# A gated update x + LN(x) y, written as one product (x - mean)(1 + rs y) with the row means put back later

## Chip, core and metric

The kernel runs on one core of a Trainium2 chip. The metric is the device time of one execution in microseconds (us), lower is better. Engines: PE (TensorE), DVE (VectorE), ACT (ScalarE), POOL (GpSimd), and SP, which only issues transfers.

## The reference, cut to what matters

Four residual layers alternate, A, B, A, B, on x of 2048 rows and 512 channels:

```python
x = A_q
x = x + _A_ref(_layernorm(x), A_k, A_v, A_shift_k, A_ssm_k, A_ssm_D)   # q * y
x = x + _B_ref(_layernorm(x), B_log_A_real, ...)                        # long convolution
x = x + _A_ref(_layernorm(x), A_k, A_v, A_shift_k, A_ssm_k, A_ssm_D)
x = x + _B_ref(_layernorm(x), B_log_A_real, ...)
```

`_layernorm` subtracts the row's mean and divides by the root of its variance plus 1e-5. `_A_ref(q, ...)` is `q * y`, where y depends on k, v and the filters and not on x, so it is the same in both A layers. `_B_ref(u, ...)` convolves u along the 2048 rows, channel by channel, with taps made from the B parameters, and adds `u * D_skip`.

So layer A is, for each row, x + (x - m) rs y with the row's mean m and rs = 1/sqrt(var + eps): a *gated update*.

## The kernel before

x lies in the on-chip memory as 16 tiles of 128 rows by 512 channels, `x[:, t, :]`. The text calls a tile a row `t`. The phases in order of time:

1. *Constants, A's y, and B's taps.* Two streams of work are interleaved. One (`diagonal`) computes A's y by long convolutions and writes it to memory (`ya_d`). The other (`taps`, `spectrum_quarter`) makes B's taps: for 64 steps an angle product on PE (L478, L483), an absolute value, a sine and a cosine on ACT (L491, L492, L493, written to tiles `tt`), products on DVE (L505, L506) and POOL (L504, L508), and a contraction on PE (L519, `pk`). Every fourth step writes taps out (L528, L529, L531, `kdram`). They are read back (L226), get D_skip added (L236), and are transformed (L171, L191, L196) into spectra `spec`, which go out from tiles `pc` (L244, L245).
2. *First gated update* (`gated_update(..., 0, True)`), which overlaps the last taps. It loads x (L701) and y (L703, tiles `yaq`, four rows each, three buffers for four loads, so the fourth load waits until the first buffer has been read).
3. *First B convolution* (`conv_b(0)`): normalised rows `u` (L770 on DVE or POOL, L773 on ACT) for one quarter of the channels at a time, forward transform on PE (L171), transposes on DVE (L189, L191), the second transform step on PE (L196, banks `pu`), whose result ACT reads out (L276, L277, tiles `sw`), products with the spectrum on DVE and POOL (L278, L280, L281), the inverse on PE (L290, L311), and the addition to x (L811, L813).
4. *Second gated update* (`gated_update(..., 1)`), which stands alone: the statistics of x end just ahead of it, and the normalisation for the next convolution follows it.
5. *Second B convolution* (`conv_b(1)`), which writes the output.

In the gated update before, each row takes a first step (x - m) y in one of three ways, chosen by a letter in WAYS1 or WAYS2: "c" is one DVE instruction (L714); "b" subtracts the mean on ACT (L717) and "d" on POOL (L719), and both then multiply by y on POOL (L720). L721 on DVE then forms ut rs + x and sums the row in the same instruction. L723 on ACT squares (sum - 512 x) and sums that, which gives the variance without another pass on DVE. `normalizer` turns the sums into nm (minus the mean), rs and nb (minus mean times rs): L208 and L209 on DVE, the root L210 on ACT, L211 to L216 on DVE. It is called once for rows 0 to 7 and once for rows 8 to 15. From row 8 on in the second update, a matmul without use (L727) keeps PE running.

The normalisation u = rs x + nb follows on three engines by letter tables (NORM1, NORM2 for the first quarter of channels, NORMQ for the second, ACT for the rest). The rows of the first three quarters are normalised before ACT reads out the first `pu`.

The order of each engine's instructions is not that of the source: a scheduler puts them in order by a simulated timeline, and each engine then works through its own list in that order. On ACT, roots, exponentials and sines need different tables; a change of kind is an ACT_TABLE_LOAD.

## Time and profile before

| | us |
|---|---|
| median of 3 runs (range) | 800.36 (798.78 to 801.9) |
| the profiled execution | 805.59 |
| its span, first to last instruction | 803.8 |
| busy in the span: PE, DVE, POOL, ACT | 635.2, 621.3, 533.7, 477.7 |
| first gated update, L717's first instruction to the last rows' normalisation | 466.1 to 523.6 |
| second gated update, first `nm` to the second `nb` | 662.3 to 693.0 |
| first read-out of `pu` (L276) behind it | 703.2 |

In the profile's rows, `out<-in` names tiles, `x8` counts instructions that were merged, and times are from the start of the span.

### The profile page before, as it was taken

The page shows a single profiled execution, that of the slowest core. Times are in us where ns is not written, and L with a number is a line of the kernel's source. Part 1 is how long each engine was busy: PE and PEld are TensorE (multiplying, and loading weights), DVE is VectorE, ACT ScalarE, POOL GpSimd, SP SyncE. Part 2 cuts the span into 40 slices and gives each one's busy share as a digit, 9 for nine tenths or more (in the row PEclk, how much of TensorE's full clock was granted, in tenths as well). Part 3 has the DMA queues.
Part 4 walks back from the last instruction along what each step waited for, and adds up shares of the span by engine and source line. Part 5 has one row for each costly group of instructions (what it writes and reads, how often), then busy time and mean ns, then how long its engine had stood idle before and what let it go on. Part 6 is the DMA issues. An engine that isn't in the chain of part 4 may idle for free. (4 is left out here: it accounts for less than half of the span.)

```text
span 803.8 us, 14448 instructions
## 1 busy us (share of the span) xinstructions
PE 635.2 (79%) x5064; PEld 447.3 (56%) x5064; DVE 621.3 (77%) x939; ACT 477.7 (59%) x879; POOL 533.7 (66%) x496
## 2 busy tenths in 40 slices
PE   3378696688799989999889863599789750998996
PEld 2255565356567747767556442386657620476673
DVE  7757979998967967647759499845668889878776
ACT  4035355345378875776785765649746525878573
POOL 4965778776778965838956277316665836288783
PEclk9676599868999999999899665789989995899999
DMA  9577177367477463664441593147987642068792
GB/s 326 188 247 270 40 241 254 108 200 254 146 215 203 127 182 110 182 171 123 115 131 34 174 341 105 46 129 199 233 200 183 159 103 54 1 164 223 201 252 105
DMA packets 89612, 135.47 MB, mean 169 GB/s; under 512 B 8508, under 2 KB 37700, under 8 KB 89028
## 3 DMA queue, kind: packets, MB, share of 16 engines
q1 hardware_dynamic: 88644, 132.13, 56.5%
q0 software_dynamic: 896, 2.43, 1.1%
q8 instruction: 40, 0.66, 0.4%
q14 instruction: 32, 0.26, 0.1%
HBM read 98.87 MB, written 35.65 MB: 167 GB/s over the span
## 5 line engine op out<-in xcount | busy, mean ns | idle before, releaser
L280 POOL TENSOR_TENSOR sw<-sw,kab 128x512 f32<-128x512 f32 x96 | 124.4, 1302 | 67.6 <-ACT sw L277 59.6
L196 PEld LDWEIGHTS pu<-zu,w 128*128 128x128 f32 x768 | 95.7, 193 | 52.9 <-DVE vv L278 18.6
L196 PE MATMUL pu<-zu,w 128*128 128x128 f32 x768 | 109.5, 285 | 15.1 <-DVE vv L278 12.8
L504 POOL TENSOR_TENSOR xy<-tt,m 128x512 f32<-128x512 f32 x64 | 84.9, 1327 | 53.5 <-ACT tt L493 23.8
L171 PE MATMUL pf<-kk,wz 128*128 128x256 f32 x256 | 86.3, 481 | 41.8 <-POOL kk L236 25.3
L278 DVE TENSOR_TENSOR vv<-pu,kab 128x512 f32<-128x512 f32 x96 | 64.9, 679 | 63.9 <-ACT sw L277 27.0
L290 PE MATMUL pi<-vv,mm 128*128 128x128 f32 x768 | 107.3, 285 | 3.5 <-DVE vv L278 2.6
L281 POOL TENSOR_TENSOR vv<-vv,sw 128x512 f32<-128x512 f32 x76 | 98.8, 1303 | 13.6 <-DVE vv L278 10.3
L290 PEld LDWEIGHTS pi<-vv,mm 128*128 128x128 f32 x768 | 96.5, 197 | 15.0 <-issue 9.1
L276 ACT ACTIVATE sw<-pu 64x512 f32<-64x512 f32 x96 | 57.0, 594 | 63.3 <-PE pu L196 60.8
L171 PEld LDWEIGHTS pf<-kk,wz 128*128 128x128 f32 x256 | 56.7, 237 | 62.3 <-POOL kk L236 33.3
L491 ACT ACTIVATE tt<-pa 128x512 f32<-128x512 f32 x64 | 38.3, 599 | 82.1 <-PE pa L483 72.3
L196 PE MATMUL pu<-zk,w 128*128 128x128 f32 x512 | 78.3, 307 | 6.4 <-DVE zk L191 4.2
L196 PEld LDWEIGHTS pu<-zk,w 128*128 128x128 f32 x512 | 72.7, 217 | 15.6 <-DVE zk L191 6.3
L505 DVE TENSOR_TENSOR tt<-tt,m 128x512 f32<-128x512 f32 x64 | 79.9, 1248 | 0.9 <-ACT tt L493 0.4
L244 ACT COPY pc<-pu 128x512 f32<-128x512 f32 x64 | 37.4, 591 | 57.3 <-PE pu L196 35.3
L506 DVE SCALAR_TENSOR_TENSOR xy<-tt,m 128x256 f32<-128x256 f32 x64 | 51.5, 805 | 25.7 <-ACT tt L492 15.3
L468 ACT ACTIVATE m<-pm 128x512 f32<-128x512 f32 x96 | 53.8, 604 | 22.6 <-PE pm L466 21.6
L483 PE MATMUL pa<-y,minus 128*128 128x512 f32 x64 | 37.1, 588 | 32.0 <-DVE y L482 30.5
L311 PE MATMUL po<-w,w 128*64 128x512 f32 x192 | 55.4, 655 | 7.3 <-DVE w L305 7.0
L519 PE MATMUL pk<-xy,tt 128*32 128x64 f32 x2048 | 50.5, 242 | 13.3 <-DVE ks L529 9.0
L519 PEld LDWEIGHTS pk<-xy,tt 128*32 128x32 f32 x2048 | 37.7, 122 | 39.1 <-issue 28.9
(139 smaller groups left out, 1295.4 us busy)
## 6 DMA issues: line engine op xcount, KB each, us to landing
kab<-spec SPq DMA_DIRECT2D x188, 256.0 KB, 4.0
spec<-pc SPq DMA_DIRECT2D x64, 256.0 KB, 2.7
kvt<-kv_in SPq DMA_DIRECT2D x16, 624.0 KB
yaq<-ya_d SPq DMA_DIRECT2D x8, 1024.0 KB, 10.6
kk<-ssmk_in SPq DMA_DIRECT2D x16, 256.0 KB, 2.9
kv_d<-u SPq DMA_DIRECT2D x16, 256.0 KB, 7.5
kdram<-ks SPq DMA_DIRECT2D x64, 64.0 KB, 1.8
kk<-kdram SPq DMA_DIRECT2D x16, 256.0 KB, 2.7
```

The lines of the kernel that those rows point to most:

```text
L171: yield T.matmul(o, w, rhs, start=True, stop=True)
L196: ins = T.matmul(pu[:, i, :], w2[:, c * CK + i, :], z[:, :, c * CK + i, :], start=True, stop=True)
L276: S.mul(sw[0:64], pu[64:128], -1.0)
L278: V.tensor_mul(vv, pu, kabs[s][:, 0])
L280: (V if last else G).tensor_mul(sw, sw, kabs[s][:, 1])
L281: (V if last or s % add_dve == add_dve - 1 else G).tensor_add(vv, vv, sw)
L290: i1s[t] = T.matmul(pi[:, i, :], mm[:, c * CK + i, :], vvs[t][:, i, :], start=True, stop=True)
L311: ins = T.matmul(po[64 * a:64 * a + 64], w4, ws[g][:, :, 16 * a:16 * a + 16, :].rearrange("p x t r -> p t x r"), start=True, stop=True, ti ...
L468: i = S.activation(m, pm, AF.Exp)
L504: G.tensor_mul(xy[:, :, :, 32:64], tt[:, :, :, 1:33], m1[:, :, 32:64][:, None].to_broadcast([128, 2, 8, 32]))
L505: (G if (4 * gi + k) % E2P == E2P - 1 else V).tensor_mul(e2, e2, m2[:, None].to_broadcast([128, 2, 8, 32]))
L519: T.matmul(pk[32 * i4:32 * i4 + 32, 2 * k + i, :], e2[:, r, 4 * i + i4, :], xy[:, r, 4 * i + i4, :], start=r == 0, stop=r == 1, tile_posit ...
```

## The change

The update is rewritten. (x - m)(1 + rs y) equals x - m + (x - m) rs y, that is, the wanted row less its mean. So per row ACT makes a factor 1 + rs y (one instruction, L718 of the changed file), and DVE makes one product (x + nm) times the factor and sums the row in the same instruction (L729). A normalisation does not see a constant added to a row, so the missing mean matters only where x itself is added to: it is collected in `off` (the sum of both updates' means) and put back once, on ACT, in the second convolution, when the third quarter's rows are due (L787, whole rows, 128x512). The third and fourth quarters are then normalised from the restored row, with a shifted nb (`nb2`, two POOL instructions).

The statistics: in the first update all 16 rows keep the square on ACT (L735). In the second, rows 0 to 7 do, and rows 8 to 15 use DVE's statistics instruction instead (L737, `BN = (16,8)`). Three factors are made ahead (`GA = 3`). The letter tables WAYS1 and WAYS2 are gone, and with them L714, L717, L719 and L720.

```diff
-    WAYS1 = "cbcdcbcdcbcdcbcd"
-    WAYS2 = "bcdbcbcbbcbbcbcb"
+    GA = 3
+    BN = (16,8)
...
+    off = cpool.tile([128, 16], F32, name="off")
...
+        groups = lambda a: a.rearrange("p (g c) -> p g c", c=32)
+        uts = {}
+        def factor(t):
+            pool, tag, bufs = spare[t % len(spare)]
+            uts[t] = pool.tile([128, 512], F32, name="ut", tag=tag, bufs=bufs)
+            S.activation(groups(uts[t]), yas[t // 4][:, :, t % 4, :], AF.Identity, scale=rs[:, t:t + 1], bias=1.0)
+
+        if rnd == 0:
+            G.tensor_scalar(off, nm, -1.0, None, op0=ALU.mult)
+        else:
+            for t0 in range(0, 16, HN):
+                G.tensor_sub(off[:, t0:t0 + HN], off[:, t0:t0 + HN], nm[:, t0:t0 + HN])
+        for t in range(GA):
+            factor(t)
         for t in range(16):
-            pool, tag, bufs = spare[t % len(spare)]
-            ut = pool.tile([128, 512], F32, name="ut", tag=tag, bufs=bufs)
-
-            groups = lambda a: a.rearrange("p (g c) -> p g c", c=32)
-            y = yas[t // 4][:, :, t % 4, :]
-            if ways[t] == "c":
-                V.scalar_tensor_tensor(groups(ut), groups(x[:, t, :]), nm[:, t:t + 1], y, op0=ALU.add, op1=ALU.mult)
+            ut = uts[t]
+            V.scalar_tensor_tensor(x[:, t, :], x[:, t, :], nm[:, t:t + 1], ut, op0=ALU.add, op1=ALU.mult,
+                                   accum_out=mv[:, t, 0:1] if t < BN[rnd] else None)
+            if t + GA < 16:
+                factor(t + GA)
+
+            if t < BN[rnd]:
+                S.activation(ut, x[:, t, :], AF.Square, scale=-512.0, bias=mv[:, t, 0:1], accum_out=mv[:, t, 1:2])
             else:
-                if ways[t] == "b":
-                    S.activation(ut, x[:, t, :], AF.Identity, bias=nm[:, t:t + 1])
-                else:
-                    G.tensor_scalar(ut, x[:, t, :], nm[:, t:t + 1], None, op0=ALU.add)
-                G.tensor_mul(groups(ut), groups(ut), y)
-            V.scalar_tensor_tensor(x[:, t, :], ut, rs[:, t:t + 1], x[:, t, :], op0=ALU.mult, op1=ALU.add,
-                                   accum_out=mv[:, t, 0:1])
-            S.activation(ut, x[:, t, :], AF.Square, scale=-512.0, bias=mv[:, t, 0:1], accum_out=mv[:, t, 1:2])
+                V.bn_stats(st0[:, t, :], x[:, t, :])
...
         def norm(c):
             for t in (2 * c, 2 * c + 1):
+                nb = nbs[0]
+                if rnd == 1 and q > 1:
+                    nb = nbs[1]
+                    if q == 2:
+                        S.activation(x[:, t, :], x[:, t, :], AF.Identity, bias=off[:, t:t + 1])
...
+    nbs.append(cpool.tile([128, 16], F32, name="nb2"))
+    G.tensor_mul(nbs[1], off, rs)
+    G.tensor_sub(nbs[1], nb, nbs[1])
     for _ in conv_b(1):
         pass
```

The scheduler's lists move with it. The rows below are instructions in an engine's own order; `xN` counts equal ones in a row. In the changed file unchanged lines have higher numbers: L210 is L213 there, L276 is L279, L491 to L493 are L494 to L496, L770 and L773 are L790 and L793.

ACT at the end of the first update, before (`tt` is a tile of cosines, L723 the squares, L210 the root):

```order
L723 ACTIVATE ut,mv<-x,mv 128x512 x2
L244 COPY pc<-pu 128x512 x2
L723 ACTIVATE ut,mv<-x,mv 128x512
L491 ACTIVATE tt_222<-pa 128x8x64
L723 ACTIVATE ut,mv<-x,mv 128x512
L492 ACTIVATE tt_222<-pa 128x8x64
L493 ACTIVATE tt_222<-tt_222,halfpi 128x8x64
L210 ACT_TABLE_LOAD
L210 ACTIVATE rs<-var 128x8
L717 ACTIVATE ut<-x,nm 128x512
L723 ACTIVATE ut,mv<-x,mv 128x512 x5
```

and in the change (L718 the factors, L735 the squares):

```order
L718 ACTIVATE ut<-yaq,rs 128x512 x2
L735 ACTIVATE ut,mv<-x,mv 128x512
L718 ACTIVATE ut<-yaq,rs 128x512
L213 ACT_TABLE_LOAD
L213 ACTIVATE rs<-var 128x8
L735 ACTIVATE ut,mv<-x,mv 128x512
L718 ACTIVATE ut<-yaq,rs 128x512
L496 ACT_TABLE_LOAD
L496 ACTIVATE tt_223<-tt_223,halfpi 128x8x64
L735 ACTIVATE ut,mv<-x,mv 128x512 x4
L793 ACTIVATE u<-x,nb,rs 128x128 x2
L213 ACT_TABLE_LOAD
```

The last cosine moved behind the first root, so the tables change three times where they changed once.

ACT from the second update's squares to the first read-out of the second convolution, before:

```order
L723 ACTIVATE ut,mv<-x,mv 128x512 x3
L210 ACTIVATE rs<-var 128x8
L723 ACTIVATE ut,mv<-x,mv 128x512 x5
L773 ACTIVATE u<-x,nb,rs 128x128 x3
L210 ACTIVATE rs<-var 128x8
L773 ACTIVATE u<-x,nb,rs 128x128 x26
L276 ACTIVATE sw<-pu 64x512
```

and in the change (L787 the means put back), from the last factors; nine more L793 and then the first L279 follow:

```order
L735 ACTIVATE ut,mv<-x,mv 128x512 x8
L718 ACTIVATE ut<-yaq,rs 128x512 x4
L213 ACTIVATE rs<-var 128x8 x2
L793 ACTIVATE u<-x,nb,rs 128x128 x3
L787 ACTIVATE x<-x,off 128x512 x4
L793 ACTIVATE u<-x,nb,rs 128x128 x10
L787 ACTIVATE x<-x,off 128x512 x3
L793 ACTIVATE u<-x,nb_6116,rs 128x128 x4
L787 ACTIVATE x<-x,off 128x512 x7
L793 ACTIVATE u<-x,nb_6116,rs 128x128 x3
L787 ACTIVATE x<-x,off 128x512 x2
```

All 16 late additions stand ahead of the first read-out, between the normalised rows.

POOL in the second update, before:

```order
L263 MEMSET kab 1x128
L719 TENSOR_SCALAR ut<-x,nm 128x512
L720 TENSOR_TENSOR ut<-ut,yaq 128x512 x10
L770 TENSOR_SCALAR u<-x,rs,nb 128x128 x8
L280 TENSOR_TENSOR sw<-sw,kab 128x512 x2
```

and in the change:

```order
L266 MEMSET kab 1x128
L724 TENSOR_TENSOR off<-off,nm 128x8 x2
L790 TENSOR_SCALAR u<-x,rs,nb 128x128 x5
L869 TENSOR_TENSOR nb_6116<-off,rs 128x16
L790 TENSOR_SCALAR u<-x,rs,nb 128x128 x3
L870 TENSOR_TENSOR nb_6116<-nb,nb_6116 128x16
L283 TENSOR_TENSOR sw<-sw,kab 128x512 x2
```

The eleven instructions on whole rows are gone, and four small ones came. The lists also differ between the two files in the taps' stage ahead of the first update, with the same instructions there but for one (`off`, on POOL).

More of the change, by code (lines that the diff above doesn't have):

```diff
@@ L705, in gated_update @@
             yas.append(ya)
[L706 to L723 removed]
+        cold = (WU1, WU2)[rnd]
+        groups = lambda a: a.rearrange("p (g c) -> p g c", c=32)
[11 more added lines that the diff above has]
+            factor(t)
+        for t in range(16):
+            ut = uts[t]
[5 more added lines that the diff above has]
+                S.activation(ut, x[:, t, :], AF.Square, scale=-512.0, bias=mv[:, t, 0:1], accum_out=mv[:, t, 1:2])
+            else:
+                V.bn_stats(st0[:, t, :], x[:, t, :])
             if t >= cold:
@@ L740, with normalized @@
     own = [(xp, "ut", 3)] * 3
-    def normalized(rows):
+    def normalized(rows, rnd):
         for t in rows:
             if t % UN == UN - 1:
-                last_root[0] = normalizer(t + 1 - UN, UN)
+                last_root[0] = normalizer(t + 1 - UN, UN, None if t < BN[rnd] else lambda i: st0[:, i, :])
     with ExitStack() as yctx:
@@ L748 @@
         normalized(gated_update(lambda k: yp.tile([128, 16, 4, 32], F32, name="yaq", tag="yaq", bufs=NYA),
-                                own + [(yp, "ut", 16 - 4 * NYA)] * (16 - 4 * NYA), 0, True))
+                                own + [(yp, "ut", 16 - 4 * NYA)] * (16 - 4 * NYA), 0, True), 0)
     bq = sbuf(ctx, "conv_q", "right")
@@ L752 @@
     turn = {"u": 0, "zu": 0}
+    nbs = [nb]
     def rotating(tag, shape, name, n):
@@ L846 @@
     normalized(gated_update(lambda k: rotating("u", [128, 16, 4, 32], "yaq", 3),
-                            own + [(pools["conv"], "vv", NSB)] * NSB + [(pools["conv"], "sw", NSB)] * NSB, 1))
+                            own + [(pools["conv"], "vv", NSB)] * NSB + [(pools["conv"], "sw", NSB)] * NSB, 1), 1)
+    nbs.append(cpool.tile([128, 16], F32, name="nb2"))
+    G.tensor_mul(nbs[1], off, rs)
+    G.tensor_sub(nbs[1], nb, nbs[1])
     for _ in conv_b(1):
```

1 line of the change is left out of this document (removed).

## The prediction

> **What bounds the kernel now.** I read the table by stage first, because the change works in two short stages and in the ScalarE queue behind the second. Its columns are the stretch, its length, the busy time of PE, weight loads, DVE, ACT and POOL with counts, the granted clock, the DMA share and GB/s.
>
> ```profile
> 465.80:523.50 57.70, 26.91 (x307) 18.18 (x306) 54.73 (x88) 32.50 (x72) 37.76 (x31) 0.65 0.50 151
> 523.50:544.40 20.90, 20.30 (x116) 17.64 (x116) 8.31 (x15) 9.84 (x21) 3.16 (x8) 0.89 0.42 132
> 662.30:690.40 28.10, 7.86 (x11) 3.06 (x12) 27.89 (x64) 17.49 (x43) 15.85 (x11) 0.53 0.18 46
> 690.40:703.20 12.80, 11.01 (x52) 5.85 (x51) 10.51 (x27) 11.62 (x33) 3.98 (x8) 1.00 0.00 1
> ```
>
> In the first gated update (row one) DVE is busy 54.73 of 57.70 us, in the second (row three) 27.89 of 28.10. Between the second update and the convolution (row four) it is ACT, 11.62 of 12.80. The chain of waits says the same: start, length, what.
>
> ```profile
> 468.57 7.37 DVE ut L714 x2
> 523.57 6.77 PE pf L171 x20
> 672.65 1.19 DVE nb L216
> 686.25 2.68 DVE x L721 x8
> 693.46 8.89 ACT u L773 x23
> ```
>
> DVE carries both updates (L714, L721); then the first of them hands over to PE at 523.57, and the second to ACT's normalisations L773. The reader should look at two lengths here. Two products of L714 took 7.37 us, and L216, an instruction on 128x8 numbers, took 1.19 us. Why, the groups show (busy us, mean ns of one | idle time before them and what ended it): four of the first update, one of the second.
>
> ```profile
> L721 DVE SCALAR_TENSOR_TENSOR x<-ut,rs,x 128x512 f32<-128x512 f32 x16 | 17.0, 1080 | 0.0
> L714 DVE SCALAR_TENSOR_TENSOR ut<-x,nm,yaq 128x512 f32<-128x512 f32 x8 | 14.9, 1899 | 0.0
> L719 POOL TENSOR_SCALAR ut<-x,nm 128x512 f32<-128x512 f32 x4 | 7.5, 1865 | 3.7 <-ACT ut L723 3.7
> L723 ACT ACTIVATE ut<-x,mv 128x512 f32<-128x512 f32 x16 | 11.5, 718 | 20.0 <-DVE x L721 19.8
> ...
> L721 DVE SCALAR_TENSOR_TENSOR x<-ut,rs,x 128x512 f32<-128x512 f32 x16 | 13.3, 866 | 0.0
> ```
>
> And in the timeline of the second update (start, length; the ACT rows give its pace):
>
> ```profile
> 662.50 1.33 ACT L717 ACTIVATE ut<-x,nm 128x512 f32<-128x512 f32 x2 [7.42 <-DVE var L209]
> 664.12 10.91 POOL L720 TENSOR_TENSOR ut<-ut,yaq 128x512 f32<-128x512 f32 x8
> 687.02 0.71 ACT L723 ACTIVATE ut<-x,mv 128x512 f32<-128x512 f32 x1
> 687.72 0.71 ACT L723 ACTIVATE ut<-x,mv 128x512 f32<-128x512 f32 x1
> 692.86 0.17 DVE L216 TENSOR_TENSOR nb<-nm,rs 128x8 f32<-128x8 f32 x1
> ```
>
> While POOL runs L720 without a pause (664.12 to 675.03), L216 needs 1.19 us; with POOL quiet it needs 0.17. The update L721 averages 1.08 and 0.87 us where four in a row take 2.68 (the chain's x8 counts their accumulator reads too), 0.67 each. So DVE is slow in the updates partly because POOL works beside it, and ACT spends 19.8 us of the first update waiting for L721.
>
> **The first update.** What ends it matters in this order:
>
> ```profile
> 502.20 0.71 ACT L493 ACTIVATE tt<-tt,halfpi 128x512 f32<-128x512 f32 x1
> 502.93 1.28 ACT L210 ACT_TABLE_LOAD   x1
> 504.22 0.21 ACT L210 ACTIVATE rs<-var 128x8 f32<-128x8 f32 x1
> 502.58 1.81 POOL L719 TENSOR_SCALAR ut<-x,nm 128x512 f32<-128x512 f32 x1
> 505.12 1.26 POOL L720 TENSOR_TENSOR ut<-ut,yaq 128x512 f32<-128x512 f32 x1 [0.74 <-ACT ut L717]
> 506.35 1.64 POOL L504 TENSOR_TENSOR xy<-tt,m 128x512 f32<-128x512 f32 x1
> 507.96 1.13 POOL L508 TENSOR_TENSOR xy<-tt,m 128x256 f32<-128x256 f32 x1
> 514.27 1.08 PE L519 MATMUL pk<-xy,tt 128*32 128x64 f32 x32
> 517.13 1.77 SPq L531 DMA_DIRECT2D kdram<-ks  x4
> 523.27 0.24 POOL L236 TENSOR_TENSOR kk<-kk,dr 1x32 f32<-1x32 f32 x1 [12.32 <-DMA kk<-kdram]
> 523.58 4.72 ACT L773 ACTIVATE u<-x,nb,rs 128x128 f32<-128x128 f32 x12 [1.15 <-DVE nb L216]
> ```
>
> These are the last steps of the kernel taps that run beside the update: the last cosine L493 ends at 502.91, its product waits on POOL behind L719 and L720 until 506.35, the contraction comes at 514.27, the taps go to memory at 517.13 and are back at 523.27. PE takes them (the chain's 523.57) at the same moment as the last normalised rows, L773. Both have to come earlier for a gain.
>
> *Removed*: 8 L714 on DVE (14.9 us), on POOL 4 L719 (7.5) and 8 L720, on ACT 4 L717. *Added*: 16 factors on ACT. A factor is L717's kind of instruction, 128x512 with one pointer operand, but reads y in 16 pieces of 32; the nearest strided one, L493, takes 0.71. Two L717 in a row take 1.33, so each further one 0.62; squares follow each other at 0.70 (687.02 to 687.72). No row reads in such pieces on ACT; I bound it by 0.6 and, with no overlap at all, 0.75, and take 0.62. Also added are two table loads, since the new order puts the root L213 between two cosines (the order is shown with the change), 1.28 each. The squares stay 16.
>
> ACT's work in the stage: 32.50 - 4 x 0.71 + 16 x 0.62 + 2 x 1.28 = 42.1 us. Behind the last cosine stand then 4 squares (2.8), 12 normalisations (4.7), one load and the roots (1.6); it can end at 465.8 + 42.1 - 9.1 = 498.8 at the earliest, and at 519 if all 19.8 us of waiting for DVE stay. DVE loses 14.9 of its 54.7 and the stalls beside 12 POOL instructions, and the squares now stand two to four together, so I take 4 us of waiting: 503, as now. What follows gets shorter: the 3.4 us that the product waits on POOL go (502.91 to 506.35), and of the 5.2 us from L508's end (509.09) to the contraction, in which DVE and POOL still interleave the update, I take 3.5. Taps 7 us earlier (bounds: 0 with the cosine at 510, 11 with it at 499). The rows: 4 squares, 2 normalisations, load, root, chain to nb (about 1) and 22 more at 0.39 end near 518 where they now end at 528.30, so they don't hold it. **First update: -7.** Behind it PE is busy 20.30 of 20.90 us and the order there is the same, so a shift is passed on. The loads of x and y don't change: SP issues them in the same order.
>
> Not covered by a row is that the scheduler also reorders the taps' stage before 466 (an extra small POOL instruction, `off`, starts it): the same instructions in another order. I take 0, with 3 us to either side, two to three DVE instructions of the slow kind (1.08).
>
> *The Trainium skill*, "ScalarE: Activation LUTs", section "What ACT_TABLE_LOAD costs", gives about 1283 ns for a load and some 1380 ns of drain besides, 2.66 us a switch. The trace agrees on the load (1.28) and shows no drain: L210's load starts 0.02 us after the cosine ends, and the root follows 0.01 us after it. By the page the two extra switches are an estimated 5.3 us instead of 2.6; it stands among the rivals.
>
> **The second update.** Rows of the timeline: the start, the chain from root to rs, the handover to the convolution, the fourth y load; then how long such a load takes to land (10.6 us), and the statistics instruction by its line.
>
> ```profile
> 662.31 0.16 DVE L209 TENSOR_SCALAR var<-mv 128x8 f32<-128x8 f32 x1
> 691.70 0.20 ACT L210 ACTIVATE rs<-var 128x8 f32<-128x8 f32 x1
> 692.62 0.21 DVE L215 SCALAR_TENSOR_TENSOR rs<-var,rs 128x8 f32<-128x8 f32 x1
> 693.06 10.11 ACT L773 ACTIVATE u<-x,nb,rs 128x128 f32<-128x128 f32 x26 [1.17 <-DVE nb L216]
> 703.19 0.59 ACT L276 ACTIVATE sw<-pu 64x512 f32<-64x512 f32 x1
> 668.51 0.37 SPq L703 DMA_DIRECT2D yaq<-ya_d  x1
> yaq<-ya_d SPq DMA_DIRECT2D x8, 1024.0 KB, 10.6
> L626 DVE BATCH_NORM_STATS2 st<-xt x16: 643/674/683, 124.5 to 190.2; 128x6 f32<-128x512 f32 x16
> ```
>
> The factor needs rs, where the old first step needed only nm. From root to rs: 691.70 to 692.83, 1.13 us. So rs is there at 662.5 + 1.13 + 0.25 (two halves interleaved) = 663.9. POOL then has only `off`, a few 128x8 instructions, hidden by its idle time. Twelve factors: 663.9 + 11 x 0.62 + 0.71 = 671.4; DVE's products follow at 0.67 and aren't late. Eight squares at 0.70: 677.0. The fourth y load goes out behind the fourth factor (666.5, today 668.51) and lands 10.6 us later, at 677.1, just when the thirteenth factor needs it. Four factors: 679.6. Then DVE is late: from the thirteenth factor (677.7) four products (2.7), four statistics at 0.67 (2.7), eight aggregations and a dozen 128x8 instructions (about 2.2, at 0.1 to 0.17 each), and five normalisations (1.5): the second nb at 686.8, today 693.03. **6.2 us earlier.**
>
> But ACT has more to do before the convolution's first eviction (L276, now 703.19): the 16 late additions, L717's form, 0.62 each, 9.9 us. Four fit into the wait for the second nb, but run over it by 1.2 us, since the three normalisations ahead start at 684.6 (684.6 + 1.2 + 2.5, less some waiting for POOL's reads of those rows: 688.0). From there 26 normalisations (10.11) and 12 additions (7.4): 705.5. **Second update: +2.3.** PE has the first products ready some 6 us earlier and waits for the eviction, so its gain is not passed on. Bounds: nb no earlier than now gives +8.6, DVE's tail done by 683 gives about -1.5. The two nb2 instructions on POOL are behind 13 ACT instructions and cost nothing; if POOL is late, ACT waits at the first u of the third quarter.
>
> **Sum.** -7 + 2.3 = -4.7: span 799.1. This profiled execution took 805.59 us with its span of 803.8, the median of the runs is 800.36; the difference goes off the median: **795.7 us**.
>
> **Rivals.** (A) The forecast, 793 to 799: 0.45; by its spread a little over half of it is under 796.4. A measurement of this kernel can tell about 0.5%, 4 us, from no change. (B) ACT hardly waits in the first update: the cosine ends at 499 to 500, taps 10 to 11 us earlier, and the second update breaks even: 790. For it: 25 us of idle ACT time (57.70 - 32.50); against it: DVE and ACT still wait for each other row by row. 0.20. (C) The first update's shift is not passed on, because PE at 20.30 of 20.90 us and the spectrum's writes set the pace, or the taps before 466 come later in the new order; half the gain goes: -3.5 + 2.3, 799. 0.13. (D) Slower: ACT becomes the bound in the first update. Place: the last cosine, behind 16 factors and two loads. If most of the 19.8 us of waiting stay, it ends at 515, 12 us later than now, the product chain is 7 shorter, so the taps come 5 later: +5 + 2.3, 807. It decides from a cosine at 510 (no gain), and is slower by 0.5% from 512 on. For it: ACT waits for DVE before nearly every square now. 0.17. (E) Each switch of tables costs another 1.28 besides the load: two more of them ahead of the last cosine are 2.6 us on the taps, 798.3. The rows at 502.93 and 504.22 speak against it. 0.05. The Trainium skill's page named above states that rule.
>
> **Chances and range.** Faster: 0.25 of A and B, 0.45. Same: 0.20 of A, C, E, 0.38. Slower: D, 0.17. The range leaves out the deeper half of B and the worse part of D: 789 to 804.5; A alone has 793 to 799.
>
> **What would show it.** Right: products near 0.74 us on DVE in the second update and 128x8 instructions near 0.17; there, counted from the first var, the second nb 24.5 us later (today 30.7) and the first eviction 43.2 (today 40.9), with ACT busy without a gap before it; and, counted from the first y load, the last taps' write 7 us earlier. Wrong: the last cosine 8 us or more later in the same count, factors over 0.75, a stage before the first update that is longer or shorter by more than 3 us, or a granted clock that falls while PE waits longer for the eviction.

## The result

Over 12 runs each the changed kernel takes a median of 794.27 us (785.87 to 802.62) and the kernel before 804.37 us (798.78 to 810.77). The ratio is 0.9851, 95% interval 0.9807 to 0.9895: 8 to 16 us less, 12.0 at the middle (0.0149 x 804.37). The ratio leaves out executions more than 1.5% above the fastest of their kernel, which is why it isn't the quotient of the two medians; the profiles of e9 and e11 below are such slow executions too, and serve only for the lengths of stages. The profiled execution of the change took 790.49 us with a span of 788.7 (before: 805.59 and 803.8).

The forecast of 795.7 us lies close to this median, but that is luck: its gain was 4.7 us, taken off a median of three runs (800.36) that was 4 us below the median of twelve.

The rest of the text counts in stages, since the whole moves from run to run more than its parts do. In the fourteen profiles of this study the first y load goes out 453.7 to 462.4 us after the start, and the first convolution (from its first read-out of `pu` to the first `var` of the second update) takes 114.3 to 120.3 us. Both differ as much between profiles whose edits don't touch them: before, e2 and e12 have the y load at 459.5, 454.0 and 453.7, and a first convolution of 118.3, 114.3 and 120.3. The lengths of the updates repeat better. In the eight profiles whose first update is the change's (the change, e1, e3, e4, e8 to e11) the taps' write comes 44.3 to 46.1 us after the y load and the first read-out of `pu` 70.1 to 72.7, so a length there is known to about 1 us; the second handover was 42.75 and, profiled again (e11), 42.77.

| stage, us | before | after |
|---|---|---|
| start to first y load | 459.46 | 457.90 |
| first y load to the last taps' write | 57.67 | 45.40 |
| first y load to first read-out of `pu` | 84.51 | 71.16 |
| first read-out to first `var` of the second update | 118.34 | 114.55 |
| that `var` to the second `nb` | 30.55 | 23.53 |
| that `var` to the first read-out behind it | 40.88 | 42.75 |
| that read-out to the end | 100.61 | 102.34 |

The two updates account for -13.35 + 1.87 = -11.5 us, which is what the ratio says. The other -3.6 of the 15.1 between the two spans lie in stages that vary by as much between profiles of equal code; of the last stage's +1.7 more is said under the clock, below.

The table by stage of the kernel before, then of the change, each row now cut exactly at these events (columns as in the prediction: stretch, length, PE, weight loads, DVE, ACT, POOL, clock, DMA share, GB/s):

```profile
459.46:517.13 57.67, 31.51 (x323) 21.91 (x323) 52.77 (x76) 33.37 (x69) 38.99 (x30) 0.62 0.58 177
662.31:692.86 30.55, 10.32 (x18) 4.25 (x19) 30.21 (x73) 18.98 (x48) 18.17 (x16) 0.57 0.16 42
703.19:717.19 14.00, 14.00 (x97) 10.33 (x95) 9.41 (x14) 10.60 (x19) 12.74 (x10) 1.00 0.70 175
```

```profile
457.90:503.30 45.40, 30.57 (x327) 20.97 (x326) 38.31 (x74) 42.06 (x85) 20.21 (x18) 0.69 0.73 225
643.61:667.14 23.53, 10.76 (x19) 4.17 (x20) 20.98 (x75) 18.25 (x41) 2.33 (x7) 0.72 0.21 56
686.36:700.36 14.00, 11.04 (x48) 8.15 (x48) 9.43 (x13) 8.19 (x14) 12.74 (x10) 0.63 0.74 170
```

In the first update DVE falls from 52.77 to 38.31 us of work and POOL from 38.99 to 20.21, ACT rises from 33.37 to 42.06, and the stage ends 12.3 us earlier. ACT has become the fullest engine, busy 42.06 of 45.40 us. In the second update POOL all but disappears (18.17 to 2.33). The last rows are the 14 us behind the handover: the granted clock of PE is 0.63 there, where it was 1.00.

The chain of waits of the change through the first update (start, length, what) names ACT where it named DVE:

```profile
493.50 0.61 ACT ut L718
494.12 1.28 ACT L213
495.53 0.80 ACT ut L735 x2
496.33 0.61 ACT ut L718
496.96 1.28 ACT L496
498.26 0.73 ACT tt L496
499.01 0.69 DVE tt L508
509.54 6.41 PE pf L171 x20
```

The timeline of the change at the end of that update (in the changed file L496 is the cosine, L507 and L511 the products on POOL, L522 the contraction, L534 the write, L213 the root):

```profile
498.26 0.72 ACT L496 ACTIVATE tt<-tt,halfpi 128x512 f32<-128x512 f32 x1
499.11 1.65 POOL L507 TENSOR_TENSOR xy<-tt,m 128x512 f32<-128x512 f32 x1 [2.45 <-issue]
500.71 0.69 POOL L511 TENSOR_TENSOR xy<-tt,m 128x256 f32<-128x256 f32 x1
501.46 0.66 PE L522 MATMUL pk<-xy,tt 128*32 128x64 f32 x32 [1.82 <-POOL xy L511]
503.13 1.28 ACT L213 ACT_TABLE_LOAD   x1
504.43 0.21 ACT L213 ACTIVATE rs<-var 128x8 f32<-128x8 f32 x1
503.30 1.77 SPq L534 DMA_DIRECT2D kdram<-ks  x4
```

The product starts 0.13 us after the cosine ends (498.98), the contraction 0.06 us after the product ends: hardly a wait is left there. Before, it took 14.2 us from the cosine's end to the write; now 4.3.

The second update and its handover in the timeline of the change (L212 is `var`, L219 `nb`, L787 the late additions, L793 the normalisation, L279 the read-out):

```profile
643.61 0.16 DVE L212 TENSOR_SCALAR var<-mv 128x8 f32<-128x8 f32 x1
667.14 0.17 DVE L219 TENSOR_TENSOR nb<-nm,rs 128x8 f32<-128x8 f32 x1
676.12 4.38 ACT L787 ACTIVATE x<-x,off 128x512 f32<-128x512 f32 x7
680.41 1.25 ACT L793 ACTIVATE u<-x,nb,rs 128x128 f32<-128x128 f32 x3
681.57 1.32 ACT L787 ACTIVATE x<-x,off 128x512 f32<-128x512 f32 x2
682.79 3.56 ACT L793 ACTIVATE u<-x,nb,rs 128x128 f32<-128x128 f32 x9
686.36 0.59 ACT L279 ACTIVATE sw<-pu 64x512 f32<-64x512 f32 x1
```

The second nb is 7.0 us earlier, and the 16 late additions take it back, and 1.9 us more.

### The profile page after: what moved, and what is told of

Read it like the earlier page. It is cut to its first block, busy times and chain, and to the rows that moved or that the text cites. A ratio compares the mean times of both kernels' runs of the same rounds, so it can differ in the third digit from the quotient of the medians.

```text
span 788.7 us, 14456 instructions
## 1 busy us (share of the span) xinstructions
PE 636.3 (81%) x5064; PEld 448.8 (57%) x5064; DVE 594.9 (75%) x933; ACT 494.0 (63%) x900; POOL 501.3 (64%) x478
## 5 line engine op out<-in xcount | busy, mean ns | idle before, releaser
L507 POOL TENSOR_TENSOR xy<-tt,m 128x512 f32<-128x512 f32 x64 | 86.8, 1356 | 63.1 <-ACT tt L496 28.9
L196 PEld LDWEIGHTS pu<-zu,w 128*128 128x128 f32 x768 | 97.2, 195 | 52.0 <-DVE vv L281 19.9
L171 PE MATMUL pf<-kk,wz 128*128 128x256 f32 x256 | 84.2, 472 | 49.1 <-POOL kk L239 34.1
L196 PE MATMUL pu<-zu,w 128*128 128x128 f32 x768 | 110.8, 287 | 15.2 <-DVE vv L281 12.8
L279 ACT ACTIVATE sw<-pu 64x512 f32<-64x512 f32 x96 | 57.0, 594 | 64.4 <-PE pu L196 62.7
L171 PEld LDWEIGHTS pf<-kk,wz 128*128 128x128 f32 x256 | 55.3, 232 | 69.5 <-POOL kk L239 37.6
L494 ACT ACTIVATE tt<-pa 128x512 f32<-128x512 f32 x64 | 38.4, 601 | 80.6 <-PE pa L486 73.6
L196 PE MATMUL pu<-zk,w 128*128 128x128 f32 x512 | 80.2, 312 | 6.3 <-DVE zk L191 4.7
L196 PEld LDWEIGHTS pu<-zk,w 128*128 128x128 f32 x512 | 74.7, 222 | 15.5 <-DVE zk L191 6.7
L508 DVE TENSOR_TENSOR tt<-tt,m 128x512 f32<-128x512 f32 x64 | 77.0, 1202 | 3.1 <-ACT tt L496 2.5
L522 PE MATMUL pk<-xy,tt 128*32 128x64 f32 x2048 | 51.0, 240 | 11.3 <-POOL xy L511 6.2
L522 PEld LDWEIGHTS pk<-xy,tt 128*32 128x32 f32 x2048 | 37.5, 120 | 34.6 <-issue 17.1
L511 POOL TENSOR_TENSOR xy<-tt,m 128x256 f32<-128x256 f32 x64 | 56.7, 886 | 0.0
```

What stands on the lines that cost most here:

```text
L171: yield T.matmul(o, w, rhs, start=True, stop=True)
L196: ins = T.matmul(pu[:, i, :], w2[:, c * CK + i, :], z[:, :, c * CK + i, :], start=True, stop=True)
L279: S.mul(sw[0:64], pu[64:128], -1.0)
L507: G.tensor_mul(xy[:, :, :, 32:64], tt[:, :, :, 1:33], m1[:, :, 32:64][:, None].to_broadcast([128, 2, 8, 32]))
L508: (G if (4 * gi + k) % E2P == E2P - 1 else V).tensor_mul(e2, e2, m2[:, None].to_broadcast([128, 2, 8, 32]))
L511: (V if (4 * gi + k) % XLP == XLP - 1 else G).tensor_mul(xy[:, 0, :, 0:32], tt[:, 0, :, 0:32], m1[:, :, 0:32])
```

## The experiments

The first theory (F): the gain is the first update's, because ACT hardly waits once DVE and POOL are relieved; the second update breaks even or loses a little, since ACT's late additions stand ahead of the first read-out. Rivals: the other order of instructions ahead of the update gave the gain (R); the second update gave it (S). A second question came with it: is it the new product that helps, or that POOL no longer works beside DVE? All lengths in one table; its columns are the stages above (y: first y load; var: the first of the second update). The unchanged parts of a kernel show how well a length repeats. Each ratio is to runs of the kernel before in the same study; their medians were 800.4 to 804.4, so that medians of different studies don't compare to better than 0.5%.

| run | median us | ratio to before (95%) | y to write | y to read-out | var to nb | var to read-out | read-out to end |
|---|---|---|---|---|---|---|---|
| before | | 1 | 57.67 | 84.51 | 30.55 | 40.88 | 100.61 |
| the change | 794.27 | 0.9851 (0.9807 to 0.9895) | 45.40 | 71.16 | 23.53 | 42.75 | 102.34 |
| e1 first update only | 793.10 | 0.9894 (0.9842 to 0.9945) | 45.40 | 71.17 | 30.55 | 40.88 | 101.24 |
| e2 second update only | 800.40 | 0.9999 (0.9960 to 1.0037) | 58.04 | 84.56 | 23.47 | 42.68 | 100.61 |
| e3 no late additions | 785.96 | 0.9834 (0.9790 to 0.9879) | 45.36 | 72.38 | 23.54 | 33.87 | 101.75 |
| e4 late additions on DVE | 787.61 | 0.9836 (0.9785 to 0.9887) | 45.34 | 70.80 | 23.56 | 41.54 | 101.54 |
| e5 useless POOL work | 808.79, one run | | 52.37 | 79.14 | 30.36 | 49.57 | 101.91 |
| e6 last cosine first | 791.12 | 0.9884 (0.9836 to 0.9932) | 45.59 | 72.19 | 23.53 | 42.75 | 100.65 |
| e7 8 squares fewer | 795.21 | 0.9913 (0.9875 to 0.9951) | 45.69 | 71.24 | 23.54 | 42.76 | 105.05 |
| e8 DVE, held back | 790.22 | 0.9865 (0.9811 to 0.9919) | 44.29 | 70.05 | 23.55 | 34.92 | 108.62 |
| e9 ACT, POOL, ACT | 787.33 | 0.9825 (0.9745 to 0.9905) | 45.40 | 71.05 | 23.91 | 36.30 | 100.94 |
| e10 ACT, POOL | 788.73 | 0.9883 (0.9829 to 0.9938) | 46.13 | 72.67 | 23.91 | 35.80 | 105.77 |
| e11 the change again | 791.68 | 0.9872 (0.9822 to 0.9922) | 44.77 | 71.77 | 23.55 | 42.77 | 100.52 |
| e12 old form, all c | 791.55 | 0.9884 (0.9839 to 0.9928) | 51.50 | 77.25 | 26.22 | 36.61 | 100.40 |

**e1 and e2: one update each.** e1 keeps the change up to the second update, which gets the old loop back; e2 is the reverse.

```diff
 # e1, against the change
+        if rnd == 1:
+            ways, cold = (WAYS1, WAYS2)[rnd], (WU1, WU2)[rnd]
+            for t in range(16):
...
+            return
-                    if q == 2:
-                        S.activation(x[:, t, :], x[:, t, :], AF.Identity, bias=off[:, t:t + 1])
 # e2, against the change
+        if rnd == 0:
+            ways, cold = (WAYS1, WAYS2)[rnd], (WU1, WU2)[rnd]
+            for t in range(16):
...
+            return
```

> The new form in the first gated update only; the second keeps the old three ways. The means are not put back (no late additions, no nb2), so the output lacks the first update's row means. Theory F (the whole gain is the first update's: ACT waits less there, the last cosine ends some 4 us earlier than before, the taps are back at PE about 12 us earlier counted from the first y load): about 12 us faster than before, ratio 0.985; first eviction 40.9 us after the first var of the second update, as before. Rival R (the gain comes mostly from the other order of the instructions ahead of the update and from the first convolution, 4 to 5 us of it): the order up to the second update is the same as in the change, so the same total, but the taps then come only 7 to 8 us earlier counted from the first y load. Rival S (the second update is what gained, since its chain got shorter): within 5 us of before.

> The new form in the second gated update only, with the late additions (off is then the second update's mean alone); the first update keeps the old three ways. Theory F: the first eviction comes 42 to 43 us after the first var (before 40.9), so +2 us, ratio 1.002, within what can be told from no change. Rival S: faster by 5 us or more. If the low clock behind the longer handover also costs (0.62 in the first 14 us behind the eviction in the changed kernel), +4.

e1 has the whole shortening of the first update (71.17) and the old second one (40.88 to the hundredth); e2 has the old first update (84.56) and the loss in the second (42.68), and its time can't be told from before. F holds, S falls. R falls too: the taps come 12.3 us earlier counted from the first y load, not 7 to 8, and the time up to that load differs as much between profiles of equal code. e1's ratio (0.9894) is weaker than F's 0.985, which its interval only just holds, and weaker than its own stages: they sum to -13.3 us, the ratio says -8.5 (-12.7 to -4.4). Where the rest went is not shown; see the reorder, below.

**e3 and e4: what the late additions cost, and DVE in place of ACT.**

```diff
 # e3
-                    if q == 2:
-                        S.activation(x[:, t, :], x[:, t, :], AF.Identity, bias=off[:, t:t + 1])
 # e4
+                nb = nbs[rnd == 1 and q > 2]
+                if rnd == 1 and q == 3 and c < 4:
+                    for r in (2 * t, 2 * t + 1):
+                        V.tensor_scalar(x[:, r, :], x[:, r, :], off[:, r:r + 1], None, op0=ALU.add)
```

> The change without its 16 late additions and without nb2; the output lacks both row means. Theory F (ACT sets the handover behind the second update): 29 normalisations in a row from the second root on end 11.3 us later, so the first eviction comes 32 to 34 us after the first var instead of 42.65, and the kernel takes 8 to 10 us less than the change, ratio to before 0.973. Rival P (PE's first products and DVE's transposes set it, as soon as ACT doesn't): eviction at 37 to 39, 4 to 5 us less than the change, ratio 0.979.

> The change with the 16 late additions on DVE instead of ACT, and written behind the third quarter's normalisations, which are made from the unrestored rows with the old nb; only the fourth quarter uses nb2. The output is complete. DVE has some 12 idle us between its last normalisations and the first eviction; 16 additions at about 0.37 (128x512 tensor_scalar instructions of the first phase take 0.36 to 0.43) are 5.9 us. Theory F: as without the additions, eviction 33 to 35 us after the first var, 7 to 9 us faster than the change, ratio to before 0.974. Rival Q (DVE's additions hold up the transposes that PE waits for): eviction at 39 to 41, 2 to 3 us faster than the change, ratio 0.982.

Without the additions the first read-out comes 33.87 us after `var`: the additions cost 8.9 us, 0.55 each, all of it on the way to the read-out. F holds for the stage. The total doesn't follow: F's 0.973 lies outside the interval of e3's 0.9834 (0.9790 to 0.9879), and the stages' -19.1 us stand against 13.3 by the ratio. With the additions on DVE 1.2 us of the 8.9 were gained, fewer even than the rival's 2 to 3. The timeline of e4 shows why (L786 the additions, L189 the transposes, L171 and L196 the two transform steps):

```profile
672.69 1.63 DVE L786 TENSOR_SCALAR x<-x,off 128x512 f32<-128x512 f32 x4
674.24 1.31 DVE L189 STREAM_TRANSPOSE zu<-pf 128x512 f32<-128x512 f32 x2
678.87 2.08 PE L171 MATMUL pf<-u,w 64*128 64x512 f32 x4 [1.10 <-DVE zu L189]
682.34 4.52 PE L196 MATMUL pu<-zu,w 128*128 128x128 f32 x24 [1.40 <-DVE zu L189]
684.46 0.59 ACT L279 ACTIVATE sw<-pu 64x512 f32<-64x512 f32 x1 [7.67 <-PE pu L196]
```

The scheduler put the additions between the transposes, as the order of DVE's instructions has it. PE waits for each pair, and ACT, which was to be relieved, waits 7.67 us for PE. Part of it, up to 3.5 us, is PE itself: its clock is 0.60 in e4's handover (666.50 to 684.46), and the two L171 groups of four took 2.08 us each and the 24 L196 4.52, where in e3 they took 1.13 and 2.95. DVE's idle time in the change was slack of a chain, not a free place.

**e5: POOL's work without its use.** The new form stays; beside it POOL multiplies constants that nobody needs.

```diff
+            way = (WAYS1, WAYS2)[rnd][t]
+            flat2 = w2.rearrange("p k c -> p (k c)")
+            if way == "d":
+                after(G.tensor_scalar(scr, flat2[:, 0:416], 2.0, None, op0=ALU.mult), f)
+            for _ in range((way != "c") + (t % 4 == 3)):
+                after(G.tensor_mul(scr, flat2[:, 0:416], flat2[:, 1024:1440]), f)
```

> The change with useless POOL work put back beside both updates (16 instructions of 128x416 in the first, 15 in the second, on constants and a scratch tile, nobody waits for their results); the rest is as in the change. Theory P (POOL's work itself slowed DVE in the old form): in the second update products at 0.87 or more instead of 0.75, 128x8 instructions near 1.2 beside POOL's work, the second nb 26 to 30 us after the first var instead of 23.5; in the first update the taps' last write 4 to 7 us later than the change's 45.4 us after the first y load. Rival Y (DVE was slow in the old form through its own instructions, above all L714 with its strided y): the second nb stays at 23.5 to 24, the write at 45.4 to 46.5.

Theory P, at the far end of its range or past it. The table by stage of e5, and one group and three rows of its second update (L738 is the product, L746 the statistics):

```profile
459.53:511.90 52.37, 33.42 (x326) 22.33 (x326) 47.37 (x75) 43.74 (x87) 40.91 (x34) 0.60 0.64 195
655.52:685.88 30.36, 10.22 (x19) 3.70 (x20) 30.03 (x76) 18.36 (x41) 22.40 (x22) 0.69 0.13 36
```

```profile
L738 DVE SCALAR_TENSOR_TENSOR x<-x,nm,ut 128x512 f32<-128x512 f32 x16 | 18.6, 1205 | 0.0
```

```profile
669.48 1.54 DVE L738 SCALAR_TENSOR_TENSOR x<-x,nm,ut 128x512 f32<-128x512 f32 x1
672.55 0.68 DVE L746 BATCH_NORM_STATS2 st<-x 128x6 f32<-128x512 f32 x1
679.54 0.73 DVE L738 SCALAR_TENSOR_TENSOR x<-x,nm,ut 128x512 f32<-128x512 f32 x1
```

No instruction waits for POOL's results, and yet DVE's product takes 1.205 us in the mean (0.748 in the change) and the second nb comes 30.36 us after `var`, as in the kernel before. While POOL works (to 677.6), nine of the sixteen products take 1.54 to 1.55 us and a statistics instruction its usual 0.62 to 0.68; behind it a product takes 0.73.

**e6 and e7: is ACT alone the bound of the first update now?**

```diff
 # e6
+                if rnd == 0:
+                    after(last_root[0], last_sin[0])
 # e7
-    BN = (16,8)
+    BN = (8,8)
```

> The change with the first root of the first update held behind the last cosine, so that the two extra table loads are gone. Theory A (ACT sets the first update in the change; it has no gaps from 469 to 502): the last cosine starts 2.8 us earlier (load, root and load, 1.28 + 0.21 + 1.28), 37.5 us after the first y load instead of 40.3, the taps' write at 42.6 instead of 45.4, the first read-out of the convolution at 68.4 instead of 71.2. Total 0.3% under the change, which the ratio can't tell. Rival D (DVE, just as full from 475 to 495, sets it): cosine and write at most 0.5 us earlier. By the Trainium skill, page ScalarE: Activation LUTs, section What ACT_TABLE_LOAD costs, with some 1.38 us of drain for a load, it would be an estimated 5.6 us instead of 2.8.

> The change with DVE's statistics instruction instead of ACT's square for rows 8 to 15 of the first update too: ACT has 8 squares less (5.6 us, of which four stand ahead of the last cosine, 2.8), DVE 8 statistics of 0.65 and 8 aggregations more (6 us). Theory A (ACT alone sets the first update in the change): cosine and taps' write 2.8 us earlier, 37.5 and 42.6 us after the first y load. Rival D (DVE is as full as ACT): write at 45 to 49, the first read-out of the convolution 0 to 3 us later than the change's 71.2.

In both the last cosine starts earlier from the first y load (38.08 and 37.55 us against 40.36), and in neither does the taps' write (45.59 and 45.69 against 45.40). Theory A holds for the cosine and falls for the stage. Rival D, which gave the cosine 0.5 us at most, is right on the write alone: ahead of the last cosine ACT and DVE are equally full, 19.98 and 19.87 us busy of the 20 from 475 to 495 in the change. In e6 the product that the cosine releases finds DVE busy (rows of its timeline; L729 the update's product, L508 the one that waits):

```profile
499.90 2.51 DVE L729 SCALAR_TENSOR_TENSOR x<-x,nm,ut 128x512 f32<-128x512 f32 x1
502.97 0.64 DVE L508 TENSOR_TENSOR tt<-tt,m 128x512 f32<-128x512 f32 x1
500.04 1.18 POOL L507 TENSOR_TENSOR xy<-tt,m 128x512 f32<-128x512 f32 x1
501.18 0.67 POOL L511 TENSOR_TENSOR xy<-tt,m 128x256 f32<-128x256 f32 x1
```

One L729 takes 2.51 us: the time of both POOL products (1.18 and 0.67) and 0.66 for itself. Nothing of e7's edit lies in the 105.05 us behind its read-out; the clock there explains them, below.

**e8, e9, e10: the late additions elsewhere.** e8 holds e4's additions behind the read-outs. e9 and e10 put rows 0 to 5 on ACT while it waits for the second root, the next six (e9) or ten (e10) on POOL, what is left (e9) on ACT as before.

```diff
 # e8, in place of the line in e4
+                        after(V.tensor_scalar(x[:, r, :], x[:, r, :], off[:, r:r + 1], None, op0=ALU.add), swapped[0])
 # e9 (RA, RP = 6, 12) and e10 (6, 16)
+            if rnd == 1 and t == 15:
+                for r in range(RA):
+                    after(S.activation(x[:, r, :], x[:, r, :], AF.Identity, bias=off[:, r:r + 1]), last_root[0])
...
+        if restored:
+            G.tensor_sub(nm[:, t0:t0 + restored], nm[:, t0:t0 + restored], off[:, t0:t0 + restored])
...
+                    if q == 2 and t < RP:
+                        G.tensor_scalar(x[:, t, :], x[:, t, :], off[:, t:t + 1], None, op0=ALU.add)
```

> As the run with the late additions on DVE, but each group of four rows held behind the read-out of its own step in the second convolution's second quarter, so that none stands among the first transposes. The output is complete. Theory: the first eviction 33.9 us after the first var, as without the additions, and the 16 additions (6.5 us on DVE, which was busy 10 to 11 of 15 us there) cost 0 to 2 us of the 101 to 102 from the eviction to the end: 7 to 9 us under the change, ratio to before 0.975. Rival: DVE's chain in the convolution is what paces it, and the additions come back in full there, 107 us from eviction to end, ratio 0.983.

> The change with its late additions taken apart: rows 0 to 5 on ACT while it waits for the second root (4.08 us idle in the change), ahead of all normalisations, whose nb for these rows is made from the shifted mean; rows 6 to 11 on POOL, which is idle from its eight normalisations (671) to the first product with the spectrum (688); rows 12 to 15 on ACT as before. The output is complete. Theory: ACT has 29 normalisations and 4 additions behind the second root, 13.8 us, so the first eviction comes 36 to 37.5 us after the first var instead of 42.75, and behind it nothing changes: 5 to 6 us under the change, ratio of the two 0.993. Rival: DVE's normalisations and 128x8 instructions slow down beside POOL's additions as they did beside L720, first eviction at 39 to 42, no gain.

> As the run with rows 6 to 11 on POOL, but rows 6 to 15 on POOL and none on ACT behind the second root. The output is complete. Theory: first eviction at 34 to 35 us after the first var; POOL's ten additions (about 1.5 us each, from 671 on in the change's times) end near 686, and the first product with the spectrum starts up to 2 us late, of which the convolution gives back most, so 6 to 8 us under the change, ratio of the two 0.991. Rival: ACT waits for POOL's rows in its normalisations of the third quarter, and the convolution takes the time back: 0 to 3 us under the change.

e8: the read-out comes at 34.92 as foreseen, and 6 to 8 us come back behind it (108.62 to the end), as the rival said. The timeline of e8:

```profile
699.14 4.32 DVE L786 TENSOR_SCALAR x<-x,off 128x512 f32<-128x512 f32 x3
```

Three additions take 4.32 us beside POOL's products, 1.44 each; ahead of the read-out, with POOL idle, e4's took 0.41.

e9 does what its theory says: 36.30 us, and nothing comes back (100.94). Its timeline, ACT and POOL (L747 the first additions on ACT, L794 five of the six on POOL):

```profile
668.44 3.77 ACT L747 ACTIVATE x<-x,off 128x512 f32<-128x512 f32 x6
678.80 7.71 POOL L794 TENSOR_SCALAR x<-x,off 128x512 f32<-128x512 f32 x5
```

Six additions fill what had been 4.08 us of idle ACT time, six more are POOL's. Of the changed kernel's 1.87 us of loss in this stage a gain of 4.6 has become. e9 has the lowest ratio that was measured with a complete output, 0.9825 (0.9745 to 0.9905), and a median 4.4 us below the change in the same study (787.33 and 791.68); the intervals of the two overlap, so that it is faster than the change is shown by the stage (6.5 us), not by the total. In e10 the read-out comes hardly earlier (35.80), and the end comes 105.77 us after it, as e10's rival had it, though at another place. POOL's additions run until 685.6, so it starts the first products with the spectrum 5.5 us after the read-out (680.13; 1.3 us in e9), and then works without a pause; beside it one product of DVE takes 6.63 us, and ACT waits (rows of its timeline).

```profile
689.37 6.63 DVE L287 TENSOR_TENSOR vv<-vv,sw 128x512 f32<-128x512 f32 x1 [0.21 <-POOL sw L286]
693.03 0.58 ACT L297 COPY ie<-pi 128x512 f32<-128x512 f32 x1 [4.47 <-PE pi L296]
```

**e11: the change again.**

> The changed kernel once more, beside the two variants on the same chip: 0.985 of before, the lengths by stage as in its first profile (13.3 us less from the first y load to the first read-out, 1.9 us more from the first var to the first eviction) within 0.3 us, while the time up to the first y load and the first convolution differ from it by up to 4 us either way, as they do between profiles of equal code.

The second update repeats to 0.02 us; the first to 0.6, not the 0.3 expected. The first convolution took 118.56 us this time. The ratio, 0.9872, is near the 0.985 expected.

**e12: the old form without POOL.** Two strings of the kernel before are changed.

```diff
-    WAYS1 = "cbcdcbcdcbcdcbcd"
-    WAYS2 = "bcdbcbcbbcbbcbcb"
+    WAYS1 = "cccccccccccccccc"
+    WAYS2 = "cccccccccccccccc"
```

> The kernel before with both letter tables all c: every first step on DVE (16 L714 instead of 8 and 6), POOL and ACT relieved of the updates' first steps; nothing else changes. Theory P (POOL's work slowed DVE more than it took off it): in the second update L714 falls from a mean of 1.30 to 0.75 and L721 from 0.87 to 0.75, 32 of them at a pace of 0.67 to 0.75 are 21.4 to 24 us, and the second nb comes 25 to 28 us after the first var instead of 30.55, although DVE has ten instructions more; in the first update L714 falls from 1.90 to about 1.1 and the first read-out of the convolution comes 0 to 4 us earlier than 84.5 us after the first y load. Rival Y (L714 is slow by itself, through its reads of y in pieces of 32): ten more of them at 1.30 are 13 us, the second nb at 38 or later, and 8 more at 1.9 in the first update, 10 us or more later there: slower than before by 2% or more.

Theory P again; in the first update it went past its range (7.3 us earlier instead of 0 to 4). The table by stage of e12, then from the second update L714's group before and two groups of e12:

```profile
453.69:505.19 51.50, 30.13 (x323) 21.06 (x323) 46.98 (x86) 33.84 (x67) 20.74 (x18) 0.60 0.65 198
651.19:677.41 26.22, 10.08 (x20) 4.63 (x20) 25.90 (x83) 13.48 (x39) 2.21 (x5) 0.60 0.15 41
```

```profile
L714 DVE SCALAR_TENSOR_TENSOR ut<-x,nm,yaq 128x512 f32<-128x512 f32 x6 | 7.5, 1295 | 0.0
```

```profile
L721 DVE SCALAR_TENSOR_TENSOR x<-ut,rs,x 128x512 f32<-128x512 f32 x16 | 11.0, 742 | 0.0
L714 DVE SCALAR_TENSOR_TENSOR ut<-x,nm,yaq 128x512 f32<-128x512 f32 x16 | 10.9, 738 | 0.0
```

With eight and ten instructions more, DVE is done sooner (first update 46.98 us of work instead of 52.77, second 25.90 instead of 30.21): L714 takes 0.738 with its strided y, as L721 does; rival Y falls. Together with e5 this makes a square, in us from the first y load to the first read-out and from `var` to the second nb:

| | with work of POOL for the update | without |
|---|---|---|
| old form | 84.51, 30.55 (before) | 77.25, 26.22 (e12) |
| new form | 79.14, 30.36 (e5) | 71.16, 23.53 (the change) |

Taking POOL off is worth 7.3 to 8.0 us in the first update and 4.3 to 6.8 in the second; the new form 5.4 to 6.1 and 0.2 to 2.7. Its price, the late additions, is 8.9. (POOL's useless work in e5 is not quite that of before: 40.91 us busy against 38.99, and 22.40 against 18.17.) The two strings gain as much as the change: -7.3 in the first update and -4.3 at the second read-out make -11.5, the same sum, and the ratio is 0.9884 (0.9839 to 0.9928), which can't be told from the change's 0.9851.

## Why the prediction was right and where it was wrong

Faster was the likeliest outcome and came, for the reasons given (DVE relieved, the chain behind the last cosine shorter, a small loss in the second update), with one term mis-sized: **the first update, forecast at -7, measured at -12.3** to the taps' write and -13.35 to the read-out. The change of each of its steps, counted from the first y load:

| step | forecast | measured |
|---|---|---|
| last cosine | 0 (4 us of waiting taken) | -2.4 |
| product's wait for POOL | -3.4 | -3.3 |
| product itself, two POOL instructions | 0 | -0.45 |
| product to contraction | -3.5 of 5.2 | -5.1 |
| contraction to write | 0 | -1.0 |
| write to read-out | 0 | -1.1 |

So the term that was mis-sized is the waiting that was left: I took 4 us on ACT and 1.7 us in front of the contraction, and there were at most 1 and 0.06. ACT worked 42.06 of 45.40 us, and of the 3.3 idle 1.57 were the wait for the first y and 0.85 one for the first angle product. The reason is in the square above, and it was found after the event. The prediction saw that DVE was slow beside POOL (1.19 against 0.17, 1.08 against 0.67), but put it into the sum as 14.9 us of L714 removed; "the stalls beside 12 POOL instructions" it named without a number, and the instructions that stay it left at their old price. They became cheaper: the one that forms the row from 1.080 (L721) to 0.839 (L729), the taps' L505 from 1.285 to 1.157 (now L508). That is close to rival B in its first half, to which 0.20 was given: counted from the y load the cosine ended at 41.1 us where B's 499 to 500 are 39.5 to 40.5, and the taps came 12.3 us earlier where B had 10 to 11. B's second half, a second update that breaks even, did not come.

The groups of the change's first update, with which the numbers just given agree:

```profile
L729 DVE SCALAR_TENSOR_TENSOR x<-x,nm,ut 128x512 f32<-128x512 f32 x16 | 13.0, 839 | 0.3 <-ACT ut L718 0.3
L718 ACT ACTIVATE ut<-yaq,rs 128x512 f32<-128x512 f32 x16 | 10.8, 732 | 1.6 <-DMA yaq<-ya_d 1.6
L508 DVE TENSOR_TENSOR tt<-tt,m 128x512 f32<-128x512 f32 x7 | 8.1, 1157 | 0.6 <-ACT tt L496 0.6
```

The 14.9 us themselves were read too evenly. L714's mean of 1.899 comes from one product of 6.78 us (row of the kernel before); the other seven average 1.20. It lasts from 469.16 to 475.94, while POOL works through seven instructions without a pause (468.80 to 475.39).

```profile
469.16 6.78 DVE L714 SCALAR_TENSOR_TENSOR ut<-x,nm,yaq 128x512 f32<-128x512 f32 x1
```

*The second update* was right: the second nb at 23.53 (forecast 24.5), the read-out at 42.75 (43.2), so +1.87 where +2.3 stood, with ACT busy without a gap ahead of it. DVE's products there were 0.748 (0.74 forecast). PE's earlier first products were not passed on, as forecast.

*The factor* kept its price: twelve in 7.46 us, a pace of 0.61; pieces of 32 cost nothing on ACT.

*The reorder ahead of the update* was taken at 0 with 3 to either side. The y load came 1.56 earlier, inside what equal code varies by. All profiles together leave it open: in the three with the old order (before, e2, e12) the load goes out at 453.7 to 459.5, in the eleven with the new one at 456.7 to 462.4. A loss of some us there, which e1's and e3's totals would fit and the change's own would not, is neither shown nor excluded.

*Rival E* falls. The root follows its load's end at 504.41 after 0.02 us, the cosine the load of 496.96 at once. The Trainium skill's page ScalarE: Activation LUTs, section What ACT_TABLE_LOAD costs, which adds about 1.38 us of drain to a load, does not describe these rows. e6 shows more: without the two extra loads the cosine comes 2.3 us earlier (2.8 were expected), and the taps don't.

*Rival C* falls in its first half: the shift was passed on, and 1.1 us more. Its second, taps that come later in the new order, is the open point just named. *Rival D* falls with the cosine; its doubt about ACT was right in that ACT is now full, which costs nothing as long as DVE is as full.

*The clock*, of which the prediction said that a fall during PE's longer wait would be a sign against it, did fall, and the fall costs time, which the forecast of the second update doesn't contain. Five profiles share the changed second update, its handover of 42.7 us and all code behind it. They differ in the clock that was granted there, and the lower it is, the later they are (us from the first read-out; the 16th and 32nd are ACT's further read-outs of `pu`, L279 and L280):

| | clock, first 14 us | 16th read-out | 32nd | end |
|---|---|---|---|---|
| before, e1, e12 (handover 36.6 to 40.9) | 1.00 | 13.95 to 13.96 | 38.5 to 38.7 | 100.4 to 101.2 |
| e2, e6, e11 | 0.76 | 15.5 to 15.6 | 38.6 to 38.7 | 100.5 to 100.7 |
| the change | 0.63 | 16.76 | 39.86 | 102.34 |
| e7 | 0.51 | 18.45 | 42.41 | 105.05 |

The stretch of e7, and two equal groups of PE in it and behind it (columns as above):

```profile
690.25:704.25 14.00, 12.04 (x33) 6.94 (x33) 8.17 (x11) 7.61 (x13) 12.15 (x10) 0.51 0.67 168
```

```profile
700.22 2.08 PE L196 MATMUL pu<-zu,w 128*128 128x128 f32 x8
711.97 1.16 PE L196 MATMUL pu<-zu,w 128*128 128x128 f32 x8
```

Eight matmuls take 2.08 us at a clock of 0.50 (694 to 702) and 1.16 at 1.00 (710 to 714), and from 694 to 706 PE works without a pause, so that its pace is what counts. At 0.76 the convolution makes up for the delay (the 4 us that e2's expectation allowed for it did not come), at 0.63 about 1.7 us of it stay, at 0.51 about 4.4. So the longer handover costs 1.87 us and, with a low clock behind it, up to 4.4 more. The profiles with a shorter handover (33.9 to 41.5 us) show 0.96 to 1.00, e5 with its 49.6 shows 0.77. Why the clock differs among the five is not shown.

What stays open: why the new form with POOL's work (e5) needs 5.4 us less than the old form with it in the first update but next to nothing less in the second. That DVE executes 16 wide products instead of 24 in the first, and 16 and 8 statistics instead of 22 in the second, fits, but wasn't tried by itself. Nearer lies the one product of 6.78 us: e2, with the same old first update, has it too (6.55), and in e5's first update no product takes more than 1.75. Above an undisturbed 0.74 that is 6.0 us, and it stands in the prediction's chain of waits (468.57). No run takes it away alone. Open, too, are the totals of e1 and e3, which gained 5 to 6 us less than their stages.

## What to carry to other kernels

Before work is shared out to POOL to relieve DVE, compare DVE's instructions beside POOL and beside an idle POOL: if they differ by more than the work handed over, take it back, which here was worth a change of two strings. When DVE or POOL is relieved, price the instructions that stay anew, not only those that go. Work that is put off must land in the idle time of a chain that nothing waits for, in the order the engine really has (e9), since idle time between two steps of a chain (e4) or at the head of a full stage (e8, e10) is given back. And where PE waits longer ahead of a full stage, look at the granted clock behind the wait: here it cost 0 to 4.4 us.

## What the runs showed of the hardware

POOL's instructions slow some of DVE's and leave others alone, whether or not there is any dependency. Beside POOL's back-to-back products a 128x512 product with two tiles as inputs took 1.54 us instead of 0.73 (e5), a 128x512 addition of a column 1.44 instead of 0.41 (e8, e4), a statistics instruction with one input 0.62 to 0.68 as ever. The Trainium skill, SBUF — State Buffer, section Who interferes with whom, has the rule: VectorE and GpSimd share one pair of ports under an exclusive lock; an instruction with two inputs in SBUF, or in a two-port mode, contends, and one with a single input outside these modes does not; whoever issues first has the pair for the whole instruction, and the other blocks. These runs agree on which instructions suffer. They differ on how long: by the page the blocked instruction waits for the one that has the ports, while in e6 a product of some 0.7 us took 2.51, past the end of one POOL instruction and through the next, and in the kernel before one took 6.78, through seven, while in e5 products and POOL's instructions took turns.
